# Small attention products gathered: three places per pair of heads, in the scores' PSUM buffers

## The chip, the cores and the metric

The kernel runs on one core of a Trainium2 chip. The metric is the device time of one execution in microseconds (us). TensorE multiplies matrices and writes only to PSUM; VectorE and ScalarE read PSUM and work on SBUF, the on-chip memory; GpSimd and the DMA queues do the rest. Each engine works through its own list of instructions in order, and semaphores make one wait for another. PSUM has eight banks of 2 KB per partition, and who may write into which bank when is what this change is about.

## The reference: what is computed

Attention in which a query sees only the keys that were assigned to the same of 16 cluster centroids, followed by a mixer block. Cut to what matters:

```python
# q, k, v: (4 batches, 8 heads, 768 tokens, 64); centroids: (8, 16, 64)
q_assign = np.argmax(np.einsum('bhsd,hcd->bhsc', q_n, c_n), axis=-1)   # normalized rows
k_assign = np.argmax(np.einsum('bhsd,hcd->bhsc', k_n, c_n), axis=-1)
mask = q_assign[:, :, :, None] == k_assign[:, :, None, :]
scores = scale * np.matmul(q, k.transpose(0, 1, 3, 2))
scores = np.where(mask, scores, -1000000000.0)
attn = np.exp(scores - np.max(scores, axis=-1, keepdims=True))
attn = attn / (np.sum(attn, axis=-1, keepdims=True) + 1e-09)
x = np.matmul(attn, v)                   # then heads side by side: (4, 768, 512)
# mixer: h = relu(x^T w_tok1) w_tok2; u = x + h^T; out = u + relu(u w_ch1) w_ch2
```

All inputs are 32-bit floats. The mixer is not touched by the change.

## The kernel before

Two heads are worked on together; there are 16 such pairs (4 batches x 4). A pair is done in 4 steps (`GROUPS`): two halves of the queries, and in each half two groups of three blocks of 128 keys. Step `m` makes the scores of its group, and the weighted values of the group of step `m - 1`. ScalarE takes the exponential of the scores in between, and VectorE adds the exponentials up (`add_up`).

Three pools lie in PSUM: `ps_sc` with three buffers of two banks for the scores, `ps_av` with one bank for the values, `ps_w` with one bank for everything small.

```python
def wtile(g, shape, dt, name):
    if g == 0:
        return ps_sc.tile(shape, dt, tag="sc", name=name)
    return ps_w.tile(shape, dt, tag="w", name=name)

def route_products(g, a0=0, a1=2):           # similarity to the centroids
    st, f = state[g], g % NF
    pr = wtile(g, [P, a1 - a0, NJ, QP], F32, "pr")
    for i in range(NQ):
        rows = slice(i * QP, (i + 1) * QP)
        nc.tensor.matmul(pr[rows], lhsT=cnd..., rhs=st["T"][:, a0:a1, :, rows]..., start=True, stop=True)

def route(g, a0=0, a1=2):                    # VectorE: the best centroid, as one-hot
    sc = rsmall.tile([P, NR, C], F32, name="sim")
    nc.vector.transpose(out=sc..., in_=st.pop("pr")...)
    nc.vector.reduce_max(out=mx, in_=sc, axis=AX.X)
    nc.vector.tensor_tensor(out=oh, in0=sc..., in1=mx..., op=ALU.is_ge)

def route_turn(g, a):                        # a = 1: keys, a = 0: queries
    po = wtile(g, [P, NJ, P], BF16, "po")
    for j in range(NJ):
        nc.tensor.transpose(out=po[:, j], in_=oh[:, a, j], identity=identb)
    # ... ScalarE copies po into st["ohT"][:, a]

def scores(m):
    scs = [ps_sc.tile([P, 2, 512], F32, tag="sc", name="sc") for _ in range(NG)]   # NG = 3
    for src, start in ((st["ohT"], True), (st["T"], False)):
        for i in range(NG):
            for h in range(2):
                nc.tensor.matmul(scs[i][:, h, 0:HS], lhsT=src[rows, 1, j0 + i], rhs=src[rows, 0, js],
                                 start=start, stop=not start)
    for i in range(NG):
        nc.scalar.activation(out=ex, in_=scs[i][:, :, 0:HS], func=ACT.Exp, scale=SM_SCALE)

def half_sums(hi):                           # den: sums of the exponentials over the keys
    den = st["den"] = ps_w.tile([P, 2 * HJ, QP], F32, tag="w", name="den")
    for i in range(NQ):
        nc.tensor.matmul(den[rows], lhsT=ones, rhs=acc[:, :, rows], start=True, stop=True)

def half_reciprocals(hi):                    # VectorE: transpose dent, then the reciprocal

def half_turn(hi):                           # px: the values of a half turned back
    px = st["px"] = ps_w.tile([P, HJ, P], F32, tag="w", name="px")
    for i in range(HJ):
        nc.tensor.transpose(out=px[:, i], in_=avT[:, i], identity=ident)

def half_out(hi):                            # VectorE: x = px * reciprocal
```

The scores are one sum in PSUM: the one-hot products come first (`ohT`, bf16; the same cluster or not), and the products of queries and keys (`T`, 32-bit) are added to them. The order of the steps:

```python
for m in range(last + 3):
    g, s = divmod(m, GROUPS)
    if half_at(m - 3) is not None: half_out(half_at(m - 3))
    if more and s == 0: turn(g + 1)
    if more and s == 1: route(g + 1)
    if 1 <= m <= last: add_up(m - 1)
    if m < last: scores(m)
    # ...
    if half_at(m - 2) is not None:
        half_sums(half_at(m - 2)); half_reciprocals(half_at(m - 2))
    if more and s == 2: route_turn(g + 1, 1)
    if 1 <= m <= last: values(m - 1)
    if half_at(m - 2) is not None: half_turn(half_at(m - 2))
    if more and s == 0: route_products(g + 1)
    if more and s == 2: route_turn(g + 1, 0)
    # ... loads of pair g + 2 at s == 1; every third m one step of preparing the weights
```

`half_at(m)` gives the number of the half that ends with step m (at s = 1 and s = 3). So a pair has seven places in TensorE's stream at which something small stands between the scores and the values: pr, den twice, px twice, po twice.

Of the kernel before, what the change touches and what calls it, by code (L numbers as in the profile page):

```python
# [8 lines left out]
F32 = mybir.dt.float32  # L9
# [3 lines left out]
ALU = mybir.AluOpType  # L13
# [3 lines left out]
B, H, S, D = 4, 8, 768, 64  # L17
C = 16
P = 128
NJ = S // P  # L20
# [6 lines left out]
HJ = NJ // 2  # L27
HS = HJ * P
WMAX = 512
# [18 lines left out]
def kernel(  # L48
# [52 lines left out]
    loads = pool("loads", 3, attention)  # L101
    small = pool("small", 2, attention)
    qktp = pool("qktp", 2, attention)
    work = pool("work", 7, attention)
    sums = pool("sums", 2, attention)

    routing = fast.enter_context(ExitStack())
    qkpool = pool("qkpool", 2, routing, side="right")
    rsmall = pool("rsmall", 2, routing, side="right")
    pools = {}  # L110


# [3 lines left out]
    cnT = const.tile([P, H * C], F32, name="cnT")  # L116
    cnd = const.tile([P, NF, 2, C], F32, name="cnd")
    ohs = [rsmall.tile([P, 2, NJ, P], BF16, name=f"oh{i}", bufs=1) for i in range(2)]
    rcps = const.tile([P, 2 * NPAIR, 2, HJ], F32, name="rcps")
    cells = const.tile([P, NPAIR], F32, name="cells")  # L120

    W = {
# [55 lines left out]
    def weight_steps(pool, W, names):  # L178

        def tmp(name, dt, n):
            return pool.tile([P, WMAX], dt, tag=name, name=name)[:, 0:n]

        def load_bits(src, p):  # L190
            n = p["n"] = src.shape[1]
            raw = pool.tile([P, WMAX, 2], U32, tag="raw", name="raw", bufs=3)[:, 0:n]
            nc.sync.dma_start(raw.rearrange("p n two -> p (n two)"), src.bitcast(U32))
            p["lo"], p["hi"] = raw[:, :, 0], raw[:, :, 1]

        def scalar_part(p):

            p["h"] = tmp("wh", U32, p["n"])
            nc.scalar.activation(out=p["h"].bitcast(F32), in_=p["hi"].bitcast(F32), func=ACT.Abs)
            p["up"] = tmp("wup", I32, p["n"])  # L200
            nc.scalar.activation(out=p["up"], in_=p["lo"], func=ACT.Copy, scale=float(2.0**-29))

        def rest(dst, p):

            h = p["h"]
            nc.vector.tensor_scalar(
                out=h.bitcast(F32), in0=h.bitcast(F32), scalar1=TINY, scalar2=HUGE,
                op0=ALU.max, op1=ALU.min,
            )

            nc.vector.tensor_scalar(
                out=h, in0=h, scalar1=0x07FFFFFF, scalar2=3,
                op0=ALU.bitwise_and, op1=ALU.logical_shift_left,
            )
            T = tmp("wT", U32, p["n"])
            nc.vector.scalar_tensor_tensor(  # L216
                out=T, in0=p["hi"], scalar=0xC0000000, in1=h,
                op0=ALU.bitwise_and, op1=ALU.bitwise_or,
            )
            T, up = T.bitcast(I32), p["up"]  # L220
            if len(dst.shape) == 3:
                T, up = (y.rearrange("t (p j) -> t p j", j=NJ) for y in (T, up))
            nc.gpsimd.tensor_tensor(out=dst.bitcast(I32), in0=T, in1=up, op=ALU.add)  # L223

        pieces = list(weight_pieces(W, names))
        parts = [{} for _ in pieces]
        for i in range(len(pieces) + 2):

            def step(i=i):
                if 2 <= i:  # L230
                    rest(pieces[i - 2][0], parts[i - 2])
                if 1 <= i <= len(pieces):
                    scalar_part(parts[i - 1])
                if i < len(pieces):
                    load_bits(pieces[i][1], parts[i])

            yield step
# [56 lines left out]
            return ps_sc.tile(shape, dt, tag="sc", name=name)  # L294
        return ps_w.tile(shape, dt, tag="w", name=name)

    def route_products(g, a0=0, a1=2):

        st, f = state[g], g % NF
        pr = wtile(g, [P, a1 - a0, NJ, QP], F32, "pr")  # L300
        for i in range(NQ):
            rows = slice(i * QP, (i + 1) * QP)
            nc.tensor.matmul(  # L303
                pr[rows], lhsT=cnd[:, f].rearrange("p i c -> p (i c)"),
                rhs=st["T"][:, a0:a1, :, rows].rearrange("p a j r -> p (a j) r"),
                start=True, stop=True,
            )
        st["pr"] = pr

    def route(g, a0=0, a1=2):  # L310

        st = state[g]
        NR = (a1 - a0) * NJ * 2
        sc = rsmall.tile([P, NR, C], F32, name="sim")
        nc.vector.transpose(
            out=sc.rearrange("p n c -> p (n c)"), in_=st.pop("pr").rearrange("p a j r -> p (a j r)")
        )
        mx = rsmall.tile([P, NR], F32, name="mx")  # L320
        nc.vector.reduce_max(out=mx, in_=sc, axis=AX.X)
        oh = ohs[g % 2][:, a0:a1].rearrange("p a j (h x) -> p (a j) h x", h=2)[:, :, :, 0:C]
        nc.vector.tensor_tensor(
            out=oh, in0=sc.rearrange("p (n h) c -> p n h c", h=2),
            in1=mx.rearrange("p (n h) -> p n h", h=2).unsqueeze(3).to_broadcast([P, NR // 2, 2, C]),
            op=ALU.is_ge,
        )
# [49 lines left out]
    def add_up(m):  # L377
# [1 line left out]
        st = state[g]  # L379
        e = [st["ex", qh, j0 + i] for i in range(NG)]  # L380
        if j0 == 0:
            acc = st["sum", qh] = sums.tile([P, 2, HS], F32, name="sum")
            nc.vector.tensor_tensor(out=acc, in0=e[0], in1=e[1], op=ALU.add)
            e = e[2:]
        acc = st["sum", qh]
        for ex in e:
            nc.vector.tensor_tensor(out=acc, in0=acc, in1=ex, op=ALU.add)  # L387

    def values(m):
# [9 lines left out]
                    start=(j == 0), stop=(j == NJ - 1),  # L399
                )  # L400
        if j0 == NJ - NG:
            st["avT", qh] = sums.tile([P, HJ, P], F32, name="avT")
            nc.scalar.copy(out=st["avT", qh].rearrange("p j t -> p (j t)"), in_=st.pop("av"))

    def half_sums(hi):

        g, qh = divmod(hi, 2)
        st = state[g]
        acc = st.pop(("sum", qh)).rearrange("p h (j t) -> p (h j) t", j=HJ)
        den = st["den"] = ps_w.tile([P, 2 * HJ, QP], F32, tag="w", name="den")  # L410
        for i in range(NQ):
            rows = slice(i * QP, (i + 1) * QP)
            nc.tensor.matmul(den[rows], lhsT=ones, rhs=acc[:, :, rows], start=True, stop=True)  # L413

    def half_reciprocals(hi):
        g, qh = divmod(hi, 2)
        dt = small.tile([P, 2 * HJ, QP], F32, name="dent")
        nc.vector.transpose(
            out=dt.rearrange("p n r -> p (n r)"),
            in_=state[g].pop("den").rearrange("p n r -> p (n r)"),  # L420
        )
        nc.vector.reciprocal(
            out=rcps[:, hi].rearrange("p h j -> p (h j)"), in_=dt[:, :, 0]
        )

    def half_turn(hi):
        g, qh = divmod(hi, 2)
        st = state[g]
        avT = st.pop(("avT", qh))
        px = st["px"] = ps_w.tile([P, HJ, P], F32, tag="w", name="px")  # L430
        for i in range(HJ):
            nc.tensor.transpose(out=px[:, i], in_=avT[:, i], identity=ident)  # L432

    def half_out(hi):

        g, qh = divmod(hi, 2)
        b, f = divmod(g, NF)
        nc.vector.tensor_tensor(  # L438
            out=xs[b][:, HJ * qh : HJ * qh + HJ, f * P : (f + 1) * P].rearrange(
                "p j (h d) -> p j h d", h=2  # L440
            ),
            in0=state[g].pop("px").rearrange("p j (h d) -> p j h d", h=2),
            in1=rcps[:, hi].rearrange("p h j -> p j h").unsqueeze(3).to_broadcast([P, HJ, 2, D]),
            op=ALU.mult,
        )
        if qh == 1:
            state.pop(g)


    turns = [0, 0]  # L450
# [220 lines left out]
    def fits():  # L671

        inside = const.tile([P, 3, 2 * NPAIR * 2 * HJ], F32, name="inside")
        good = const.tile([P, 3], F32, name="good")
        flat = rcps.rearrange("p n h j -> p (n h j)")
        for i, (limit, op) in enumerate(((LIMIT, ALU.is_le), (1.0 / LIMIT, ALU.is_ge))):
            nc.vector.tensor_scalar(
                out=inside[:, i], in0=flat, scalar1=limit, scalar2=None, op0=op
# [57 lines left out]
    begin()  # L736
    weights = list(weight_steps(stage, W, ("tok1", "tok2", "ch1")))
    last = NPAIR * GROUPS
    HALF = GROUPS // 2
    ends = [lambda t=t: tok1(0, t) for t in range(NT)]  # L740
    for b in range(B):
        if b + 1 < B:
            ends += [lambda b=b, t=t: tok1(b + 1, t) for t in range(NT)]
        ends += [lambda b=b, j=j: tok2(b, j) for j in range(NJ)]

    def half_at(m):

        return m // HALF if 0 <= m < last and m % HALF == HALF - 1 else None

    for m in range(last + 3):  # L750
        g, s = divmod(m, GROUPS)
        more = g < NPAIR - 1
        if half_at(m - 3) is not None:
            half_out(half_at(m - 3))
        if more and s == 0:
            turn(g + 1)
        if more and s == 1:
            route(g + 1)
        if 1 <= m <= last:
            add_up(m - 1)  # L760
        if m < last:
            scores(m)
        if m == last:
            ps_sc_stack.close()
            pools["ps_m"] = pool("ps_m", 2, space=PSUM)
        if half_at(m - 2) is not None:
            half_sums(half_at(m - 2))
            half_reciprocals(half_at(m - 2))
        if more and s == 2:
            route_turn(g + 1, 1)  # L770
        if 1 <= m <= last:
            values(m - 1)
        if half_at(m - 2) is not None:
            half_turn(half_at(m - 2))
        if more and s == 0:
            route_products(g + 1)
        if more and s == 2:
            route_turn(g + 1, 0)
        if s == 1 and g + 2 < NPAIR:
            load(g + 2)  # L780
        if m == last - GROUPS:
# [254 lines left out]
```

## Time and profile before

| | |
|---|---|
| time, median of 3 runs | 913.79 us (911.97 to 915.61) |
| span of the profiled execution | 914.3 us |
| granted TensorE clock, mean | 0.994 |
| VectorE busy | 507.3 us, 55% of the span |
| exponentials, 192 of 128 x 768 | 141.8 us busy, 812 ns each |
| sums of the exponentials, 128 + 32 of 128 x 768 | 130.1 + 30.4 us busy |
| den, 256 records of 192 columns | 17.0 us busy |
| px, 96 transposes | 17.5 us busy |
| po, 192 transposes | 17.0 us busy |
| pr, 120 records of 384 columns | 12.8 us busy |

How to read it. The page gives for each engine the time in which it was busy. Matmuls are pipelined, so the duration of one record overlaps the next; the length of a stretch of TensorE work is best read as the distance from its start to the start of what follows. A 32-bit product appears as two records. In the timeline the last bracket of a line tells how long the engine had been idle before it and what ended the wait. Shapes such as 64\*128 are the rows and columns of the array that a product uses.

### The profile page before, as it was taken

To read this page: it belongs to the slowest core of one execution; us is meant where nothing else is said; L and a number is where in the kernel's file an instruction comes from. 1 tells how busy PE (TensorE), PEld (TensorE's weight loads), DVE (VectorE), ACT (ScalarE), POOL (GpSimd) and SP (SyncE) were. 2 spreads that over 40 slices of the span, in tenths; PEclk is the share of its full clock that TensorE was granted. 3 is DMA by queue.
4 is the path that set the end of the run, shared out by engine and by line. 5 is a ranking of instruction groups with operands and counts; after the bars stand their busy time and mean duration, and the time that the engine had idled before them with its cause. 6 is when DMAs were issued, how large, how long until landed. Compare 5 with 4: busy or idle time off the path is not lost.

```text
span 914.3 us, 11630 instructions
## 1 busy us (share of the span) xinstructions
PE 895.6 (98%) x4594; PEld 533.6 (58%) x4594; DVE 507.3 (55%) x851; ACT 303.5 (33%) x515; POOL 45.0 (5%) x40
## 2 busy tenths in 40 slices
PE   7999999999999999999999899999999999999997
PEld 3444444444444444444458568677686876858676
DVE  5787787787787875577463244333443334433342
ACT  2655565565565654231130121211212012130210
POOL 1000010010010100131000000000000000000000
PEclk9999999999999999999999899999999999999999
DMA  9725426325334100240000001000010000100001
GB/s 154 157 54 107 82 70 109 80 75 99 76 85 89 62 27 1 65 143 1 0 1 1 0 1 47 23 1 1 0 47 24 0 1 12 47 12 1 1 12 61
DMA packets 112830, 41.76 MB, mean 46 GB/s; under 512 B 101632, under 2 KB 105728, under 8 KB 112768
## 3 DMA queue, kind: packets, MB, share of 16 engines
q1 hardware_dynamic: 109632, 40.55, 19.4%
q10 hardware_dynamic: 3136, 0.39, 0.4%
q8 instruction: 38, 0.62, 0.3%
q14 instruction: 24, 0.20, 0.1%
HBM read 34.64 MB, written 6.29 MB: 45 GB/s over the span
## 4 chain that ended last, share of the span: by engine, by line
PE 92%; DVE 5%; DMA 1%; issue 1%; ACT 0%; DVEq 0%
PE sc L368 16%; PE pX L652 14%; PE pX L601 14%; PE av L397 13%; PE pZ L652 7%; PE pZ L601 7%; PE ph L470 5%; PE pu L479 5%; PE pY L652 3%; PE pY L601 3%; PE px L432 2%; DVE sum L387 2%; PE po L341 2%; PE den L413 1%; PE pr L303 1%; PE pt L542 1%
## 5 line engine op out<-in xcount | busy, mean ns | idle before, releaser
L374 ACT ACTIVATE ex<-sc 128x768 f32<-128x768 f32 x192 | 141.8, 812 | 117.5 <-PE sc L368 117.5
L397 PE MATMUL av<-ex,va 128*64 128x384 f32 x768 | 138.0, 494 | 0.0
L387 DVE TENSOR_TENSOR sum<-sum,ex 128x768 f32<-128x768 f32 x128 | 130.1, 1016 | 10.1
L368 PE MATMUL sc<-qkT 64*128 64x384 f32 x768 | 134.3, 482 | 0.0
L368 PEld LDWEIGHTS sc<-qkT 64*128 64x128 f32 x768 | 71.4, 187 | 38.0
L397 PEld LDWEIGHTS av<-ex,va 128*64 128x64 f32 x768 | 49.4, 136 | 66.2 <-issue 59.8
L601 PE MATMUL pX<-uT,wc 128*128 128x384 f32 x192 | 68.8, 495 | 1.6 <-issue 1.6
L609 ACT COPY p<-pX 128x384 f32<-128x384 f32 x24 | 11.4, 475 | 153.1 <-PE pX L601 153.1
L601 PEld LDWEIGHTS pX<-uT,wc 128*128 128x128 f32 x192 | 36.7, 193 | 26.7 <-issue 3.3
L223 POOL TENSOR_TENSOR wc<-wT,wup 128x512 int32<-128x512 int32 x24 | 32.4, 1349 | 251.2 <-DVE wT L216 251.2
L368 PE MATMUL sc<-ohT 64*128 64x384 bf16 x384 | 42.6, 327 | 0.6 <-DVE ohT L344 0.6
L479 PE MATMUL pu<-h,wt 128*128 128x512 f32 x96 | 42.0, 592 | 0.0
L470 PE MATMUL ph<-x,wt 128*128 128x512 f32 x96 | 42.0, 593 | 0.0
L496 DVE TENSOR_TENSOR x<-pX,x 128x256 f32<-128x256 f32 x24 | 10.2, 424 | 55.1 <-PE pX L652 55.1
L496 DVE TENSOR_TENSOR c<-pZ,u 128x384 f32<-128x384 f32 x24 | 13.4, 557 | 46.8 <-PE pZ L601 46.8
L652 PE MATMUL pX<-w2s,hA 128*128 128x256 f32 x144 | 36.4, 390 | 0.5 <-DVE x L496 0.5
L438 DVE TENSOR_TENSOR x<-px,rcps 128x384 f32<-128x384 f32 x32 | 17.8, 556 | 33.5 <-PE px L432 33.5
L496 DVE TENSOR_TENSOR hA<-pY,p 128x384 f32<-128x384 f32 x24 | 13.4, 557 | 40.4 <-PE pY L601 40.4
L652 PE MATMUL pX<-wc,hA 128*128 128x256 f32 x144 | 35.0, 379 | 0.0
L601 PE MATMUL pZ<-uTs,w1s 128*128 128x384 f32 x96 | 35.0, 487 | 0.0
L652 PE MATMUL pX<-w2s,hS 128*128 128x256 f32 x144 | 35.0, 379 | 0.0
L652 PE MATMUL pZ<-wc,hS 128*128 128x256 f32 x144 | 35.0, 379 | 0.0
(115 smaller groups left out, 1227.0 us busy)
## 6 DMA issues: line engine op xcount, KB each, us to landing
raw<-in_moe_w_ch_dram SPq DMA_DIRECT2D x24, 512.0 KB, 3.9
qk<-in_k_dram SPq DMA_DIRECT2D x64, 96.0 KB, 4.4
va<-in_v_dram SPq DMA_DIRECT2D x16, 384.0 KB, 3.3
out_dram<-x SPq DMA_DIRECT2D x24, 256.0 KB, 2.0
qk<-in_q_dram SPq DMA_DIRECT2D x60, 96.0 KB, 3.6
raw<-in_moe_w_tok_dram SPq DMA_DIRECT2D x3, 512.0 KB, 5.8
raw<-in_moe_w_tok_dram SPq DMA_DIRECT2D x4, 384.0 KB, 4.2
qk<-in_q_dram ACTq DMA_DIRECT2D x4, 96.0 KB, 4.8
```

What stands on the lines that cost most here:

```text
L223: nc.gpsimd.tensor_tensor(out=dst.bitcast(I32), in0=T, in1=up, op=ALU.add)
L341: nc.tensor.transpose(out=po[:, j], in_=oh[:, a, j], identity=identb)
L368: nc.tensor.matmul(scs[i][:, h, 0:HS], lhsT=src[rows, 1, j0 + i], rhs=src[rows, 0, js], start=start, stop=not start,)
L374: nc.scalar.activation(out=ex, in_=scs[i][:, :, 0:HS], func=ACT.Exp, scale=SM_SCALE)
L387: nc.vector.tensor_tensor(out=acc, in0=acc, in1=ex, op=ALU.add)
L397: nc.tensor.matmul(st["av"][h * D : (h + 1) * D], lhsT=st["va"][:, h, j], rhs=ex[:, h], start=(j == 0), stop=(j == NJ - 1),)
L432: nc.tensor.transpose(out=px[:, i], in_=avT[:, i], identity=ident)
L470: nc.tensor.matmul(pf, lhsT=W["tok1"][:, j, t * P : (t + 1) * P], rhs=xs[b][:, j], start=(j == 0), stop=(j == NJ - 1),)
L479: nc.tensor.matmul(pu, lhsT=W["tok2"][:, t, j], rhs=h1s[b][:, t], start=(t == 0), stop=(t == NT - 1))
L496: nc.vector.tensor_tensor(out=dst, in0=a, in1=b, op=ALU.add)
L601: nc.tensor.matmul(psum, lhsT=A[a][:, k, c * P : (c + 1) * P], rhs=R[r][:, k], start=start and k == 0, stop=k == 1, skip_group_check=not s ...
L652: nc.tensor.matmul(psum, lhsT=h2[a][:, k, i * P : (i + 1) * P], rhs=Bw[w][:, 3 * part + k], start=start and k == 0, stop=k == 2, skip_grou ...
```

## The change

The small products of a pair are put together, each for the whole pair, and in three places: den and pr side by side after the values of step 1, px (six transposes) and the keys' po after the values of step 2, the queries' po after the values of step 3. The den and pr pair takes one of the three score buffers (two banks: one each), and px takes one too. It is meant to spare TensorE the changes between small and large products, VectorE and ScalarE some instructions, and to free the small products from the single bank of `ps_w`. The room for whole pairs in SBUF comes from fewer work buffers (6 for 7), single buffers in the routing scratch and a single `wT`.

```diff
-    work = pool("work", 7, attention)
+    work = pool("work", 6, attention)
-    rsmall = pool("rsmall", 2, routing, side="right")
+    rsmall = pool("rsmall", 1, routing, side="right")
 ...
+            bufs = 1 if name == "wT" else 2
 ...
-    def route_products(g, a0=0, a1=2):
+    def route_products(g, a0=0, a1=2, pr=None):
-        pr = wtile(g, [P, a1 - a0, NJ, QP], F32, "pr")
+        if pr is None:
+            pr = ps_sc.tile([P, (a1 - a0) * NJ * QP], F32, tag="sc", name="pr")
 ...
+    def pair_sums(g, den):
+        acc = st.pop("sum").rearrange("p i h (j t) -> p (i h j) t", j=HJ)
         for i in range(NQ):
             nc.tensor.matmul(den[rows], lhsT=ones, rhs=acc[:, :, rows], start=True, stop=True)
+    def pair_reciprocals(g):      # one transpose of 384 columns, one reciprocal of 12
+    def pair_turn(g, px):         # six transposes, three into each bank
+    def pair_out(g):              # two products, one per bank
 ...
     for m in range(last + 3):
         g, s = divmod(m, GROUPS)
+        old = g - 1 if m < last else -1
+        if s == 3 and old >= 0:
+            pair_out(old)
         if more and s == 0:
             turn(g + 1)
-        if more and s == 1:
-            route(g + 1)
+        if s == 2:
+            if old >= 0:
+                pair_reciprocals(old)
+            if more:
+                route(g + 1)
         if 1 <= m <= last:
             add_up(m - 1)
         if m < last:
             scores(m)
+        if 1 <= m <= last:
+            values(m - 1)
+        if m < last and s == 1:
+            both_w = ps_sc.tile([P, 2, 512], F32, tag="sc", name="small")
+            if old >= 0:
+                pair_sums(old, both_w[:, 0, 0:HS])
+            if more:
+                route_products(g + 1, pr=both_w[:, 1, 0:HS])
+        if m < last and s == 2:
+            if old >= 0:
+                px = ps_sc.tile([P, 2, 512], F32, tag="sc", name="px")
+                pair_turn(old, [px[:, i, 0:HS] for i in range(2)])
+            if more:
+                route_turn(g + 1, 1)
+        if more and s == 3:
+            route_turn(g + 1, 0)
 ...
+        if m == last + 1:         # the last pair: sums, reciprocals and turn, in ps_w and ps_av
```

The half-wise calls of before are taken out.

More of the change, by code (lines that the diff above doesn't have):

```diff
@@ L118 @@
     ohs = [rsmall.tile([P, 2, NJ, P], BF16, name=f"oh{i}", bufs=1) for i in range(2)]
-    rcps = const.tile([P, 2 * NPAIR, 2, HJ], F32, name="rcps")
+    rcps = const.tile([P, NPAIR, 2, 2, HJ], F32, name="rcps")
     cells = const.tile([P, NPAIR], F32, name="cells")
@@ L187, in tmp @@
         def tmp(name, dt, n):
-            return pool.tile([P, WMAX], dt, tag=name, name=name)[:, 0:n]
+            bufs = 1 if name == "wT" else 2
+            return pool.tile([P, WMAX], dt, tag=name, name=name, bufs=bufs)[:, 0:n]
         def load_bits(src, p):
@@ L317, in route @@
         nc.vector.transpose(
-            out=sc.rearrange("p n c -> p (n c)"), in_=st.pop("pr").rearrange("p a j r -> p (a j r)")
+            out=sc.rearrange("p n c -> p (n c)"), in_=st.pop("pr")
         )
@@ L381, in add_up @@
         if j0 == 0:
-            acc = st["sum", qh] = sums.tile([P, 2, HS], F32, name="sum")
+            if qh == 0:
+                st["sum"] = sums.tile([P, 2, 2, HS], F32, name="sum")
+            acc = st["sum"][:, qh]
             nc.vector.tensor_tensor(out=acc, in0=e[0], in1=e[1], op=ALU.add)
             e = e[2:]
-        acc = st["sum", qh]
+        acc = st["sum"][:, qh]
         for ex in e:
@@ L401, in values @@
         if j0 == NJ - NG:
[L402 to L407, printed above, removed]
+            if qh == 0:
+                st["avT"] = sums.tile([P, NJ, P], F32, name="avT")
+            js = slice(HJ * qh, HJ * qh + HJ)
+            nc.scalar.copy(out=st["avT"][:, js].rearrange("p j t -> p (j t)"), in_=st.pop("av"))
+    def pair_sums(g, den):
         st = state[g]
-        acc = st.pop(("sum", qh)).rearrange("p h (j t) -> p (h j) t", j=HJ)
-        den = st["den"] = ps_w.tile([P, 2 * HJ, QP], F32, tag="w", name="den")
+        acc = st.pop("sum").rearrange("p i h (j t) -> p (i h j) t", j=HJ)
+        st["den"] = den
         for i in range(NQ):
@@ L413, in half_sums @@
             nc.tensor.matmul(den[rows], lhsT=ones, rhs=acc[:, :, rows], start=True, stop=True)
[L415 to L420, printed above, removed]
-        )
[L422 to L432, printed above, removed]
@@ L434, in half_out @@
-    def half_out(hi):
-        g, qh = divmod(hi, 2)
-        b, f = divmod(g, NF)
[L438 to L447, printed above, removed]
+    def pair_reciprocals(g):
+        dt = small.tile([P, 4 * HJ, QP], F32, name="dent", bufs=1)
+        nc.vector.transpose(out=dt.rearrange("p n r -> p (n r)"), in_=state[g].pop("den"))
+        nc.vector.reciprocal(
+            out=rcps[:, g].rearrange("p i h j -> p (i h j)"), in_=dt[:, :, 0]
+        )
@@ new lines, in pair_turn @@
+    def pair_turn(g, px):
+        avT = state[g].pop("avT")
+        for i in range(NJ):
+            nc.tensor.transpose(
+                out=px[i // HJ][:, (i % HJ) * P : (i % HJ) * P + P], in_=avT[:, i], identity=ident
+            )
+        state[g]["px"] = px
+    def pair_out(g):
+        b, f = divmod(g, NF)
+        px = state[g].pop("px")
+        for qh in range(2):
+            nc.vector.tensor_tensor(
+                out=xs[b][:, HJ * qh : HJ * qh + HJ, f * P : (f + 1) * P].rearrange(
+                    "p j (h d) -> p j h d", h=2
+                ),
+                in0=px[qh].rearrange("p (j h d) -> p j h d", h=2, j=HJ),
+                in1=rcps[:, g, qh].rearrange("p h j -> p j h").unsqueeze(3)
+                .to_broadcast([P, HJ, 2, D]),
+                op=ALU.mult,
+            )
+        state.pop(g)
@@ L674, in fits @@
         good = const.tile([P, 3], F32, name="good")
-        flat = rcps.rearrange("p n h j -> p (n h j)")
+        flat = rcps.rearrange("p n i h j -> p (n i h j)")
         for i, (limit, op) in enumerate(((LIMIT, ALU.is_le), (1.0 / LIMIT, ALU.is_ge))):
@@ L738 @@
     last = NPAIR * GROUPS
-    HALF = GROUPS // 2
     ends = [lambda t=t: tok1(0, t) for t in range(NT)]
@@ L744 @@
         ends += [lambda b=b, j=j: tok2(b, j) for j in range(NJ)]
-    def half_at(m):
-        return m // HALF if 0 <= m < last and m % HALF == HALF - 1 else None
     for m in range(last + 3):
@@ L752 @@
         more = g < NPAIR - 1
-        if half_at(m - 3) is not None:
-            half_out(half_at(m - 3))
+        old = g - 1 if m < last else -1
+        if s == 3 and old >= 0:
+            pair_out(old)
         if more and s == 0:
             turn(g + 1)
-        if more and s == 1:
-            route(g + 1)
+        if s == 2:
[3 more added lines that the diff above has]
+                route(g + 1)
         if 1 <= m <= last:
@@ L765 @@
             pools["ps_m"] = pool("ps_m", 2, space=PSUM)
[L766 to L778, printed above, removed]
+        if m == last + 1:
+            pair_sums(NPAIR - 1, ps_w.tile([P, HS], F32, tag="w", name="den"))
+            pair_reciprocals(NPAIR - 1)
+            pair_turn(
+                NPAIR - 1,
+                [
+                    ps_w.tile([P, HS], F32, tag="w", name="px"),
+                    ps_av.tile([P, HS], F32, name="av"),
+                ],
+            )
+        if m == last + 2:
+            pair_out(NPAIR - 1)
         if s == 1 and g + 2 < NPAIR:
```

## The prediction

> **What bounds the kernel now.** I read the page's busy shares first, then its chain of waits, then the timeline of one head pair in the middle of the attention, with the engines TensorE, VectorE and ScalarE kept side by side. From the page:
>
> ```profile
> span 914.3 us, 11630 instructions
> PE 895.6 (98%) x4594; PEld 533.6 (58%) x4594; DVE 507.3 (55%) x851; ACT 303.5 (33%) x515; POOL 45.0 (5%) x40
> ...
> PE 92%; DVE 5%; DMA 1%; issue 1%; ACT 0%; DVEq 0%
> ```
>
> TensorE is busy 98% of the span and is 92% of the chain that ended last. So time is won only by giving TensorE less to do or fewer gaps, and every wait put into its stream is paid in full. The change touches only the attention, 15.8 to about 367 us. The timeline of one pair (start, duration, engine, line, output and input):
>
> ```profile
> 212.33 2.10 PE L368 MATMUL sc<-qkT 64*128 64x384 f32 x12
> ...
> 214.36 2.16 PE L397 MATMUL av<-ex,va 128*64 128x384 f32 x12
> ...
> 216.44 0.85 PE L303 MATMUL pr<-qkT,cnd 128*32 128x384 f32 x8
> ...
> 217.23 0.66 PE L368 MATMUL sc<-ohT 64*128 64x384 bf16 x6
> ...
> 218.72 0.57 DVE L317 STREAM_TRANSPOSE sim<-pr 128x384 f32<-128x384 f32 x1
> ...
> 219.75 0.53 PE L413 MATMUL den<-sum,ones 128*32 128x192 f32 x8
> ...
> 220.22 2.16 PE L397 MATMUL av<-ex,va 128*64 128x384 f32 x12
> ...
> 222.91 0.55 PE L432 MATMUL px<-ident,avT 128*128 128x128 f32 x3 [0.54 <-DVE dent L418]
> ...
> 223.39 0.66 PE L368 MATMUL sc<-ohT 64*128 64x384 bf16 x6
> ...
> 225.92 0.51 PE L341 MATMUL po<-identb,oh 128*128 128x128 bf16 x6
> ...
> 226.36 2.16 PE L397 MATMUL av<-ex,va 128*64 128x384 f32 x12
> ...
> 228.44 0.51 PE L341 MATMUL po<-identb,oh 128*128 128x128 bf16 x6
> ...
> 228.89 0.66 PE L368 MATMUL sc<-ohT 64*128 64x384 bf16 x6
> 228.99 0.80 ACT L346 COPY ohT<-po 128x768 bf16<-128x768 bf16 x1
> 229.38 2.10 PE L368 MATMUL sc<-qkT 64*128 64x384 f32 x12
> ...
> 232.01 0.38 DVE L418 STREAM_TRANSPOSE dent<-den 128x192 f32<-128x192 f32 x1 [3.04 <-PE den L413]
> ...
> 232.43 0.19 DVE L422 RECIPROCAL rcps<-dent 128x6 f32<-128x6 f32 x1
> ...
> 234.55 0.56 DVE L438 TENSOR_TENSOR x<-px,rcps 128x384 f32<-128x384 f32 x1 [0.38 <-PE px L432]
> ```
>
> The reader takes from it the start-to-start lengths on TensorE, which carry everything below: one-hot scores 0.50 (228.89 to 229.38), score products 2.03 (212.33 to 214.36), value products 2.08 (214.36 to 216.44), pr 0.79, den 0.47, px 0.48, po 0.44. TensorE goes from each to the next without a gap; the one it shows, 0.54 before px, is the VectorE's dent, and the same list for all pairs has three such gaps of 0.6 and one of 0.17, about 2 us in all. Two more things: no small product is followed at once by something that needs its result (the copy ohT at 228.99 is for scores that start a whole step later), and VectorE starts 0.04 to 0.07 after a TensorE group ends.
>
> **What the Trainium skill says.** "TensorEngine Tiling (Array Packing)", Key Properties: changing the tiling mode drains TensorE. The trace agrees: three px transposes follow each other every 0.11, yet the place costs 0.48, so about 0.15 lies in going in and out; po is 6 x 0.057 = 0.34 and costs 0.44. The third column of shapes gives four modes (64*128 scores, 128*64 values, 128*32 pr and den, 128*128 px and po). "TensorE: Matmul & The Clock Gate", Part 3, The mechanism: matmuls are strictly first in, first out; only weight loads are pulled ahead. So a matmul that waits for a buffer stops all behind it. "Perfetto Trace Analysis", Optimizing Tensor Performance, Matmuls: independent groups should rotate through PSUM banks so that emptying one lies beside the next group. Before, the three score buffers do just that (no wait in the trace); the change puts more work with slower readers into that rotation.
>
> **The change part by part.** A pair has four steps, s = 0 to 3, each scores, then values of the step before.
> Removed: the mode switches. Before, the four steps have 3+4+4+4 = 15 switches, after 2+3+3+3 = 11. The columns streamed are the same: den was twice 192 and is once 384, px twice 3 transposes and now 6. Step lengths after, without waits: s0 0.50+2.03+2.08 = 4.61; s1 adds den with 384 columns ahead of pr in the same mode (0.65, estimated from pr's 0.79 less the switch) and pr 0.79 = 6.05; s2 adds six transposes (about 0.75) and po 0.44 = 5.80; s3 adds po 0.44 = 5.05. Sum 21.5, against before 4 x 4.61 + 0.79 + 2 x 0.47 + 2 x 0.48 + 2 x 0.44 = 22.0. Saved about 0.48 a pair, 7 us over 15 pairs, and the 2 us of dent waits: 9 us.
>
> Added: three waits on TensorE in each pair.
> (A) den and pr lie in one score buffer, and the next scores use the three buffers in rotation, so their third tile takes that one and waits until VectorE has read both halves. In the order of instructions the transpose dent waits for TensorE and the transpose sim for nothing: dent's wait already covers the end of pr. From den's start: pr starts at 0.65 and ends at 1.50; dent 1.57 to 2.15 (384 columns: 0.58 by the sim row); reciprocal until 2.38, the next starts 0.1 after it began; sim 2.30 to 2.88; TensorE goes on at 2.94. Without the wait it reaches the third tile at 0.65 + 0.79 + 2/3 of 0.50 = 1.77. Wait 1.2.
> (B) px lies in a score buffer too, read by two products of 0.56; the first waits for all six transposes. From px's start: transposes end 0.82, products 0.87 to 1.92, TensorE goes on at 1.98; without it 0.75 + 0.44 + 0.33 = 1.52. Wait 0.45. VectorE comes to it just in time (after sim: maximum 0.55, one-hot 0.6, three sums 3.05, so 7.2 from den's start; px ends about 8.1), except in the five pairs whose weight step falls in s2: its three operations (0.42 + 0.43 + 0.69) push it 0.6 later, wait 1.05.
> (C) po for the queries moves from s2 to the end of s3, and the next step on TensorE is the next pair's scores, which need its copy as moving operand. po ends 0.51 after its start, ScalarE (idle then, the exponentials are done 1 us earlier) copies from 0.55 to 1.35, scores start at 1.40 in place of 0.44. Wait 0.96.
>
> Sum: A 14 full pairs x 1.2, and 0.45 each for the first (no den) and last (no pr) = 17.7; B 9 x 0.45 + 5 x 1.05 + 0.85 for the last pair, which has no po to cover it = 10.2; C 15 x 0.96 = 14.4. Together 42.3. Saved 9. The last pair's sums and turn now come whole after the loop, 0.65 more streamed and a 0.2 longer dent: 0.8. Net +34: 913.8 + 34 = 948; I take 947, as the first reader may overlap more than I let it.
>
> Not on the path: one work buffer less (ScalarE's exponentials then wait for sums two steps back, done in time by the times above), single buffers in the routing scratch (one engine's own order) and in the weight scratch (a step every 3 steps), fewer VectorE and ScalarE instructions (both have idle time in the pair: VectorE was busy 17.5 of 22.6).
>
> **Rivals.** (1) The mode switches are worth more than I think and the waits lie under slack: then 905. For it: it is what the change is meant for. Against: TensorE has no slack anywhere in the pair, and C is a plain chain of TensorE, ScalarE, TensorE that nothing can fill, 14 us alone. (2) Only C hurts, because dent starts as soon as den ends and px's first product after three transposes. Then A falls to about 0.65 and B to 0.1 to 0.6: 10 + 4 + 14 - 8 = +20, 934. Against it: the missing waits on the second reader. (3) VectorE becomes the bound: its work per pair is about 19.5 with a weight step and the pair gets 24 long, so no; it would show as waits of ScalarE for VectorE and give 960 or more. (4) The gaps of about 1 us make the clock fall. The Trainium skill, "TensorE: Matmul & The Clock Gate", Part 1, What's actually happening, puts the idle window at about 3.4 us, and the gaps are a third of that; in the trace the granted clock is 1.00 all through the attention, also with the gap of 0.54. Unlikely, and worth 50 us or more.
>
> **Range and chances.** The low end, 934, is rival 2; the high end, 960, has 0.15 more for each of some 43 resumptions after a wait (6 us), or VectorE late in more pairs. Faster by 2% (below 895.5) would need the whole account to be wrong: 0.02. Within 2% (to 932): only if two of the three waits are nearly nothing: 0.08. Slower: 0.90.
>
> **What would show it.** The timeline of a middle pair should be 24.0 to 24.8 long in place of 22.6; the one-hot scores at s0 should start 1.4 after po with an idle of about 0.9 put down to the ScalarE copy; in the one-hot group at s2 an idle of about 1.2 put down to sim, at s3 one of 0.5 to 1.1 put down to the output product. Matmul busy time should fall by some 7 us while idle grows by about 42. If TensorE shows no idle before the scores at s0, step C is wrong; if dent starts before pr has ended, step A; if po and px side by side still cost 1.3 together, the switch saving.

## The result and the profile after

The changed kernel takes 946.89 us (median of 6, 945.95 to 948.74) against 914.62 us (6 runs of the kernel before): ratio 1.0358, 95% interval 1.0339 to 1.0376. It is slower by 32.3 us, and the prediction said 947. From the page of the changed kernel, the span, the busy time of each engine, and the shares of the chain that ended last:

```profile
span 945.0 us, 11319 instructions
...
PE 891.6 (94%) x4466; PEld 533.4 (56%) x4466; DVE 498.9 (53%) x819; ACT 305.6 (32%) x515; POOL 44.7 (5%) x40
...
PE 89%; DVE 7%; ACT 2%; DMA 1%; issue 1%; DVEq 0%
```

TensorE's busy time fell by 4.0 us, and still the span grew by 30.7: TensorE's share fell from 98% to 94%, and VectorE and ScalarE rose from 5% and 0% of the chain to 7% and 2%. Nothing new is computed; TensorE waits. For whom, the list of waits of the changed kernel says (who waits, for whom: us in total, times, longest):

```profile
PE sc L370 <- DVE sim L319: 13.9, 15, 1.0
...
PE sc L370 <- ACT ohT L348: 13.3, 15, 0.9
...
PE sc L370 <- DVE x L441: 7.8, 15, 0.9
```

These are three waits, each in 15 pairs, all before one-hot products of the scores; the kernel before has none of them. The timeline of a pair in the middle shows each at its place (start, duration, engine, line, operation; in brackets the idle time before, and what ended it). `small` is the buffer that den and pr share, `sc<-ohT` are the one-hot products, `av` the values:

```profile
239.04 0.85 PE L418 MATMUL small<-sum,ones 128*32 128x384 f32 x8
...
239.71 0.83 PE L305 MATMUL small<-qkT,cnd 128*32 128x384 f32 x8
...
240.47 0.50 PE L370 MATMUL sc<-ohT 64*128 64x384 bf16 x4
240.61 0.58 DVE L422 STREAM_TRANSPOSE dent<-small 128x384 f32<-128x384 f32 x1 [4.95 <-PE small L305]
241.23 0.23 DVE L423 RECIPROCAL rcps<-dent 128x12 f32<-128x12 f32 x1
241.37 0.52 DVE L319 STREAM_TRANSPOSE sim<-small 128x384 f32<-128x384 f32 x1
...
241.95 0.34 PE L370 MATMUL sc<-ohT 64*128 64x384 bf16 x2 [0.98 <-DVE sim L319]
...
246.24 0.88 PE L431 MATMUL px<-ident,avT 128*128 128x128 f32 x6
...
246.95 0.50 PE L343 MATMUL po<-identb,oh 128*128 128x128 bf16 x6
247.15 1.02 DVE L441 TENSOR_TENSOR x<-px,rcps 128x384 f32<-128x384 f32 x2 [1.08 <-PE px L431]
...
247.38 0.50 PE L370 MATMUL sc<-ohT 64*128 64x384 bf16 x4
...
248.23 0.34 PE L370 MATMUL sc<-ohT 64*128 64x384 bf16 x2 [0.35 <-DVE x L441]
...
252.52 0.51 PE L343 MATMUL po<-identb,oh 128*128 128x128 bf16 x6
...
253.06 0.80 ACT L348 COPY ohT<-po 128x768 bf16<-128x768 bf16 x1 [1.58 <-PE po L343]
...
253.91 0.66 PE L370 MATMUL sc<-ohT 64*128 64x384 bf16 x6 [0.89 <-ACT ohT L348]
```

Wait A: den and pr follow each other; four of the six one-hot products run (240.47), then the last two stand until VectorE has read both halves of the buffer (sim ends at 241.89). They start at 241.95, 1.48 after the first four, where they are due after 0.33: 1.15 lost. Wait B: after px and po the same four run (247.38), and the last two stand for the two output products: 0.85 in place of 0.33, 0.52 lost. Wait C: po starts at 252.52, ScalarE's copy runs from 253.06 to 253.86, and the next pair's scores start at 253.91, 1.39 after po in place of 0.44: 0.95 lost.

A pair, from one den to the next, is 24.10 us long, in five of the pairs 24.5 to 24.6; the kernel before has 22.01 for most. In the five longer ones VectorE comes late to the output products, since three operations of a weight step stand ahead of them:

```profile
197.62 0.88 PE L431 MATMUL px<-ident,avT 128*128 128x128 f32 x6
...
198.35 0.69 DVE L217 SCALAR_TENSOR_TENSOR wT<-raw,wh 128x512 uint32<-128x512 uint32 x1
198.96 1.02 DVE L441 TENSOR_TENSOR x<-px,rcps 128x384 f32<-128x384 f32 x2
...
200.03 0.34 PE L370 MATMUL sc<-ohT 64*128 64x384 bf16 x2 [0.77 <-DVE x L441]
```

px is done at 198.50 there, but the output products start at 198.96, right behind the weight step, and TensorE's idle is 0.77 in place of 0.35. From the first scores to the first product of the mixer the attention takes 383.41 us against 351.71: 31.7 us more, where the profiled spans differ by 30.7.

### The profile page after: what moved, and what is told of

It reads as the page before. It is cut to its first block, busy times and chain, and to the rows that moved or that the text cites. A ratio compares the mean times of both kernels' runs of the same rounds, so it can differ in the third digit from the quotient of the medians.

```text
span 945.0 us, 11319 instructions
## 1 busy us (share of the span) xinstructions
PE 891.6 (94%) x4466; PEld 533.4 (56%) x4466; DVE 498.9 (53%) x819; ACT 305.6 (32%) x515; POOL 44.7 (5%) x40
## 4 chain that ended last, share of the span: by engine, by line
PE 89%; DVE 7%; ACT 2%; DMA 1%; issue 1%; DVEq 0%
PE sc L370 15%; PE pX L655 13%; PE pX L604 13%; PE av L401 13%; PE pZ L655 7%; PE pZ L604 7%; PE ph L473 4%; PE pu L482 4%; PE pY L655 3%; PE pY L604 3%; DVE x L441 2%; DVE sum L391 1%; ACT ohT L348 1%; PE small L418 1%; PE small L305 1%; PE pt L545 1%
## 5 line engine op out<-in xcount | busy, mean ns | idle before, releaser
L391 DVE TENSOR_TENSOR sum<-sum,ex 128x768 f32<-128x768 f32 x128 | 125.1, 978 | 10.6 <-ACT ex L376 0.5
L370 PE MATMUL sc<-ohT 64*128 64x384 bf16 x384 | 48.4, 329 | 36.4 <-DVE sim L319 13.9
L370 PEld LDWEIGHTS <-ohT 64*128 64x128 bf16 x384 | 15.6, 94 | 73.0 <-issue 34.7
L422 DVE STREAM_TRANSPOSE dent<-small 128x384 f32<-128x384 f32 x15 | 8.7, 583 | 76.4 <-PE small L305 71.2
L387 DVE TENSOR_TENSOR sum<-ex 128x768 f32<-128x768 f32 x32 | 32.4, 1012 | 15.7 <-ACT ex L376 15.6
L655 PE MATMUL pZ<-w2s,hS 128*128 128x256 f32 x144 | 35.0, 379 | 0.0
L655 PE MATMUL pY<-wc,hA 128*128 128x256 f32 x144 | 35.0, 379 | 0.0
```

Of the source, the lines that this page charges most:

```text
L655: nc.tensor.matmul(psum, lhsT=h2[a][:, k, i * P : (i + 1) * P], rhs=Bw[w][:, 3 * part + k], start=start and k == 0, stop=k == 2, skip_grou ...
```

## The experiments

A pair length below is the distance from the start of one pair's den (or pr) to that of the next in the timeline. The times of the kernel before, run beside each group of kernels, were 913.71 to 915.51 us.

**One wait taken away at a time.** Each of the next three moves one block of small products from behind the values of its step to between scores and values. Work, buffers and mode switches stay; the values (2.08 us) now lie between the product and whoever needs its buffer or copy.

```diff
         if m < last:
             scores(m)
+        if more and s == 3:            # c_early; a_early: the den/pr block; b_early: px and po
+            route_turn(g + 1, 0)
         if 1 <= m <= last:
             values(m - 1)
 ...
-        if more and s == 3:
-            route_turn(g + 1, 0)
```

The queries' po early (wait C):

> The changed kernel with one move: the queries' po of step 3 stands between the scores and the values of that step instead of after the values. Same products, same number of mode switches. Theory (wait C is a plain chain TensorE, ScalarE copy, TensorE with nothing beside it): the 2.08 us of values now cover the copy, 15 x 0.95 = 14.3 us go, so 932.5 us. Rival (the loss comes from the larger products and the switches, the idle only shows where they end): within 3 us of 947.

Measured 933.26 us (ratio to before 1.0207, 1.0183 to 1.0230); pairs of 23.14, each 0.96 shorter. Waits A and B stay as they were (13.9 and 7.8 us). C is the plain chain.

den and pr early (wait A):

> The changed kernel with one move: den and pr of step 1 stand between scores and values instead of after the values. Theory: the values cover dent, reciprocal and sim, wait A goes (14 x 1.15 and two of 0.4, about 17 us). VectorE also gets through with sim 2 us earlier, so that the five output products delayed by a weight step come in time: about 2 us of wait B more. 927 to 930 us. Rival (a buffer taken out of the rotation costs the same wherever its products stand): no gain over 3 us, the idle moves to another tile of the scores.

Measured 927.11 us (1.0144, 1.0127 to 1.0162). All pairs are 22.95: 1.15 shorter, and the five long ones are gone too, as VectorE is through with sim earlier.

px and the keys' po early (wait B):

> The changed kernel with one move: px and the keys' po of step 2 stand between scores and values. Theory: the values cover the two output products where VectorE is on time, wait B goes in ten pairs; in the five pairs with a weight step on VectorE ahead of them the products come so late (px itself is earlier now) that about 1 us of wait stays. 4 to 6 us gained: 941 to 943 us. Rival (wait B is the two products alone): all of its 10 us go, 937 us.

Measured 941.2 us (1.0296, 1.0275 to 1.0316). Nine of the fourteen distances from den to den are 23.6, 0.53 shorter; five stay at 24.5 to 24.6. The list of waits of this kernel:

```profile
PE sc L370 <- DVE sim L319: 13.9, 15, 1.0
PE sc L370 <- ACT ohT L348: 13.3, 15, 0.9
...
PE sc L370 <- DVE x L441: 3.9, 5, 0.9
```

The wait for the output product x is down from 15 times to 5. These five are the pairs in which VectorE comes late; the two products alone are not the whole of wait B, and the rival's 937 us is out.

**All three at once.**

> All three moves at once: every small product stands between the scores and the values of its step. Theory: the three waits lie in series on TensorE and all are covered, what stays is the saving of four mode switches a pair (0.5 us x 15) and of the 2 us of dent waits of the kernel before: 905 us, faster than both kernels. Rival (VectorE, with about 19.5 us of work per pair, becomes the bound once a pair takes 21.5 us): 910 to 918 us, with waits of TensorE or ScalarE for VectorE in the pairs with a weight step.

Measured 904.33 us (0.9894, 0.9876 to 0.9913): faster than both. One pair in its timeline:

```profile
212.74 0.85 PE L418 MATMUL small<-sum,ones 128*32 128x384 f32 x8
...
213.41 0.83 PE L305 MATMUL small<-qkT,cnd 128*32 128x384 f32 x8
...
214.16 2.16 PE L401 MATMUL av<-ex,va 128*64 128x384 f32 x12
214.30 0.58 DVE L422 STREAM_TRANSPOSE dent<-small 128x384 f32<-128x384 f32 x1 [1.90 <-PE small L305]
...
215.06 0.52 DVE L319 STREAM_TRANSPOSE sim<-small 128x384 f32<-128x384 f32 x1
...
216.25 0.66 PE L370 MATMUL sc<-ohT 64*128 64x384 bf16 x6
...
218.78 0.88 PE L431 MATMUL px<-ident,avT 128*128 128x128 f32 x6
...
219.49 0.50 PE L343 MATMUL po<-identb,oh 128*128 128x128 bf16 x6
219.69 1.02 DVE L441 TENSOR_TENSOR x<-px,rcps 128x384 f32<-128x384 f32 x2
...
219.92 2.16 PE L401 MATMUL av<-ex,va 128*64 128x384 f32 x12
...
222.01 0.66 PE L370 MATMUL sc<-ohT 64*128 64x384 bf16 x6
...
224.54 0.51 PE L343 MATMUL po<-identb,oh 128*128 128x128 bf16 x6
...
224.97 2.16 PE L401 MATMUL av<-ex,va 128*64 128x384 f32 x12
...
225.45 0.82 ACT L348 COPY ohT<-po 128x768 bf16<-128x768 bf16 x1
...
227.06 0.66 PE L370 MATMUL sc<-ohT 64*128 64x384 bf16 x6
```

After each small product the values (av) start at once, VectorE or ScalarE empties the buffer beside them, and the scores start 2.09 after the values, with no idle of TensorE in a bracket. Pairs are 21.47 to 21.56 long. The three moves alone gain 13.6, 19.8 and 5.7 us, 39.1 together; all at once gain 42.6. Most of the difference lies in the five pairs in which B's move alone gained nothing: with A's move as well, 0.53 is gained in each of them, 2.7 us. VectorE as a bound is out: TensorE has no wait for it left in the pairs.

**Is it the shared buffer? pr back in the small bank.** Only the place of pr changes; den stays in the score buffer, behind the values.

```diff
-            both_w = ps_sc.tile([P, 2, 512], F32, tag="sc", name="small")
-            if old >= 0: pair_sums(old, both_w[:, 0, 0:HS])
-            if more: route_products(g + 1, pr=both_w[:, 1, 0:HS])
+            if old >= 0:
+                den_w = ps_sc.tile([P, 2, 512], F32, tag="sc", name="small")
+                pair_sums(old, den_w[:, 0, 0:HS])
+            if more: route_products(g + 1, pr=ps_w.tile([P, HS], F32, tag="w", name="pr"))
```

> The changed kernel with pr of step 1 in the single small bank, as before the change, and den alone in the score buffer; nothing is moved in time. Theory (dent waited for the end of pr because both lie in one buffer, and TensorE for both readers): dent starts 0.07 us after den's end in place of pr's end and is read before the third score tile needs the buffer, so the idle put down to sim goes from 0.98 to nothing, 17 us gained; VectorE is not much earlier with its sums, TensorE comes 1.15 us earlier to px, so wait B grows by some 0.6 in the five pairs with a weight step: 930 to 934 us. Rival (the wait is the restart of TensorE after small products): the idle at the third tile stays above 0.5.

Measured 932.39 us (1.0192, 1.0177 to 1.0208). From its timeline:

```profile
208.33 0.85 PE L418 MATMUL small<-sum,ones 128*32 128x384 f32 x8
...
209.00 0.83 PE L305 MATMUL pr<-qkT,cnd 128*32 128x384 f32 x8
...
209.25 0.58 DVE L422 STREAM_TRANSPOSE dent<-small 128x384 f32<-128x384 f32 x1 [3.64 <-PE small L418]
...
209.76 0.66 PE L370 MATMUL sc<-ohT 64*128 64x384 bf16 x6
...
210.01 0.52 DVE L319 STREAM_TRANSPOSE sim<-pr 128x384 f32<-128x384 f32 x1
```

dent starts 0.92 after den and no longer 1.57, before pr has ended (209.83), and the six one-hot products are one unbroken piece of 0.66. Without the common buffer the wait is gone with den behind the values as before, so it was the two readers of one buffer and no restart cost. Pairs are 22.95, the five late ones 23.87: wait B grew there from 0.94 to about 1.44, as expected.

**Wait C by itself, in the kernel before.**

```diff
-        if more and s == 2:
+        if more and s == 3:
             route_turn(g + 1, 0)
```

> The kernel before the change with one part of the change alone: the queries' po made at the end of step 3 and not of step 2. Theory: wait C by itself, 15 x 0.95 = 14 us, less about 0.1 a pair because px and po now stand side by side in one mode: 926 to 928 us. Rival (in the kernel before there is slack that hides it): 914 to 918 us.

Measured 937.63 us (1.0254, 1.0238 to 1.0270): 10 us more than expected. The timeline shows a wait I had left out:

```profile
222.99 0.55 PE L432 MATMUL px<-ident,avT 128*128 128x128 f32 x3
...
223.58 0.56 DVE L438 TENSOR_TENSOR x<-px,rcps 128x384 f32<-128x384 f32 x1 [1.93 <-PE px L432]
...
224.19 0.49 PE L341 MATMUL po<-identb,oh 128*128 128x128 bf16 x6 [0.65 <-DVE x L438]
...
224.72 0.80 ACT L346 COPY ohT<-po 128x768 bf16<-128x768 bf16 x1 [3.23 <-PE po L341]
225.57 0.66 PE L368 MATMUL sc<-ohT 64*128 64x384 bf16 x6 [0.89 <-ACT ohT L346]
```

At 225.57 stands wait C with its 0.89, as in the changed kernel. Ahead of it, po waits 0.65 for the output product of VectorE (line 438): px and po share the one small bank there. The follow-up gives the queries' po a score buffer (`wtile` takes one for g = 0):

```diff
-        po = wtile(g, [P, NJ, P], BF16, "po")
+        po = wtile(g if a else 0, [P, NJ, P], BF16, "po")
```

> The kernel before the change with the queries' po at the end of step 3, as in the last look at it, but po in a score buffer in place of the single small bank. Theory (of the 23 us lost there, some 10 are po waiting in that bank for the output product to read px, seen as an idle of 0.65 before po; the rest is wait C): the idle before po goes, 0.95 - 0.1 a pair stays, 926 to 929 us. Rival (moving po to the end of step 3 costs 1.5 us a pair wherever it lies): 936 us or more.

Measured 924.62 us (1.0104, 1.0088 to 1.0119), pairs of 22.85: 22.01 + 0.95 for C - 0.10 for px and po in one mode give 22.86. The time is below the expected range. In part this is so because the waits for dent of the kernel before (2 us, three pairs of 22.61 and one of 22.18) are gone in this kernel, which I had not counted: the attention is 10.5 us longer than before, as 15 x 0.85 - 2.0 = 10.7 says. The rest of the shortfall lies outside the attention and was not taken apart. The single bank was indeed a bottleneck for products put close together, and the change was right to fear it.

**The smaller SBUF buffers.** In the kernel before:

```diff
-    work = pool("work", 7, attention)
+    work = pool("work", 6, attention)
-    rsmall = pool("rsmall", 2, routing, side="right")
+    rsmall = pool("rsmall", 1, routing, side="right")
+            bufs = 1 if name == "wT" else 2
```

> The kernel before the change with the change's smaller buffers alone: 6 work buffers for 7, single buffers in the routing scratch, one wT. Theory: none of them is waited for on the way to TensorE, 914 us, within 1. Rival (the exponentials wait for the sums two steps back): 916 us or more, with ScalarE waiting for VectorE.

Measured 915.37 us against 914.43 (ratio 1.0005, 0.9997 to 1.0014). No cost shows; by the interval it is 1.3 us at most.

**The five long pairs.** In the changed kernel, weight steps that fall into step 2 put off to step 3.

```diff
-            n = m % WEVERY == 0 or m == 1
+            n = (m % WEVERY == 0 and s != 2) or (m % WEVERY == 1 and s == 3) or m == 1
```

> The changed kernel with the weight steps that fall into step 2 put off to step 3 of the same pair; same work. Theory (in five of the pairs, 24.5 us long in place of 24.1, the three weight operations on VectorE stand ahead of the output products): all pairs 24.1 us long, 2.1 us less in all, 944 to 945.5 us. Rival (the weight loads or ScalarE's part of the step are in the way): the five longer pairs stay, or others become longer.

Measured 944.54 us (1.0321, 1.0305 to 1.0337), and all pairs are 24.10. It was the weight step. This run moves ScalarE's part of the step too; that VectorE's part was in the way is read from the lines above, in which the output products start right behind the last of its three operations.

**What a mode switch costs.** From all three moves, the keys' po of step 2 back behind the values, so that px and po stand apart:

```diff
         if m < last and s == 2:        # px, between scores and values
-            if more:
-                route_turn(g + 1, 1)
 ...
             values(m - 1)
+        if more and s == 2:
+            route_turn(g + 1, 1)
```

> All three moves, but the keys' po of step 2 after the values, so that px and po stand apart: one mode switch more a pair, nothing else. Theory (a switch costs 0.10 to 0.15 us, read from px 0.71 ahead of po and 0.81 ahead of scores): 1.5 to 2.2 us more than with all three moves. Rival (switches cost nothing and the saving came from waits): the same time.

Measured 906.56 us (0.9904, 0.9889 to 0.9920), beside 904.33 (0.9894, 0.9876 to 0.9913): the intervals overlap, the times alone do not tell. The pairs do: 21.57 or 21.58 in all of them, 0.10 to 0.11 more than 21.47. The cost is there, and small. Whether it belongs to the change of mode or to one more separate place as such, these runs do not tell apart; below it is called the cost of a switch.

**One place less still.** Both po after px in step 2, in a score buffer of their own, no small product in step 3:

```diff
-            if more:
-                route_turn(g + 1, 1)
-        if more and s == 3:
-            route_turn(g + 1, 0)
+        if more and s == 2:
+            pos = ps_sc.tile([P, 2, 1024], BF16, tag="sc", name="po")
+            for a in (1, 0):           # turn into pos[:, a], and ScalarE's copy
+                route_turn(g + 1, a, pos[:, a, ...])
```

> All three moves, and both po of a pair right after px in step 2, in a score buffer of their own, so that step 3 has no small product: one mode switch less a pair (10 in place of 11). Theory (a switch is 0.10 us): pairs of 21.36 in place of 21.47 us, 1.5 us less, 902 to 904 us. Rival (two of the three score buffers are now away at once, and the scores of step 3 wait for ScalarE's two copies): longer pairs, 906 to 915 us, with TensorE waiting for the copy ohT at step 3.

Measured 920.95 us (1.0062, 1.0047 to 1.0076): neither. TensorE does wait for the copy, but not at step 3:

```profile
208.03 0.50 PE L344 MATMUL po<-identb,oh 128*128 128x128 bf16 x6
...
208.56 0.81 ACT L351 ACTIVATE ohT<-po 128x768 bf16<-128x768 bf16 x1 [0.20 <-PE po L344]
...
209.51 0.49 PE L344 MATMUL po<-identb,oh 128*128 128x128 bf16 x6 [0.99 <-ACT ohT L351]
```

The second po waits until ScalarE has copied the first (208.56 to 209.37), because both lie in one buffer and I had written turn, copy, turn, copy. It is wait A again, in the writing direction: each half is 2 KB, a bank of its own, but in this program the writer of one half waits for the reader of the other. With all twelve turns ahead of the two copies:

```diff
-            for a in (1, 0):
-                route_turn(g + 1, a, pos[:, a, ...])
+            for a in (1, 0): route_turn(g + 1, a, po[a], copy=False)
+            for a in (1, 0): route_turn(g + 1, a, po[a], turn=False)
```

> As the last look at two places, but all twelve po transposes come before ScalarE's two copies. Theory (the wait of 0.99 before the second po came only from both po lying in one buffer whose first half ScalarE was reading): that wait goes, pairs of 21.36 us, 15 x 0.1 us less than with all three moves, 902 to 904 us. Rival (the copies, both now after the second po, hold the third score tile of step 3): a wait for the copy ohT at step 3, 905 us or more.

Measured 902.84 us (0.9876, 0.9855 to 0.9898), all pairs 21.36: the shortest pairs of the study, by the 0.11 of one switch. The interval overlaps that of all three moves; the pairs tell the two apart.

## Why the prediction was right

Point by point:

- *The gain from fewer places* was put at 0.48 us a pair. A pair with its three waits subtracted is 24.10 - 1.15 - 0.52 - 0.95 = 21.48, and with the waits really gone it is 21.47; before it was 22.01. The gain is 0.54. (The prediction's own step lengths give 22.01 - 21.51 = 0.50.) The parts: den to pr 0.67 (predicted 0.65), px to po 0.71 (0.75), pr to scores 0.76 (0.79).
- *Wait A*, 1.2 predicted, 1.15 measured. That dent would wait for the end of pr was read from the order of instructions, and shown by pr in its own bank.
- *Wait B*, 0.45 and 1.05 predicted, 0.52 and 0.94 measured. The five late pairs and their cause were right.
- *Wait C*, 0.96 predicted, 0.95 measured, alone in the kernel before as well.
- *The sum*, 42.3 predicted: 14 x 1.15 + 2 x 0.43 + 9 x 0.52 + 4.8 + 0.85 + 15 x 0.95 = 41.5. Here 0.43 is A in the first and the last pair, 4.8 is B in the five late ones, 0.85 B in the last.
- *Not on the path*: the smaller buffers, shown in the kernel before.
- *The clock*: the granted clock reads 1.00 over the attention of the changed kernel, as before; gaps of about 1 us three times in 24 did not lower it.

What was off: I said that busy time would fall by 7 us and idle grow by 42. The profile shows 4.0 (2.4 of it in the attention) and, by the list of waits, 35.0. A matmul's record reaches past the start of the next, so where the stream stops in the middle of the one-hot products, 0.17 of the stop still counts as busy (0.98 of idle for 1.15 lost). The working by start-to-start distances was not touched by it. And a small wait was missed: the second step of the first pair now follows the first with nothing between, and meets exponentials that are not done, two idles of 0.15 and 0.36. The 22.6 named as the pair before is the pair shown there, with its gap of 0.54; most are 22.01. Of the 0.8 for the last pair nothing can be seen: from the first product of the mixer to the end it is 546.5 us against 546.8, at a granted clock of 1.00 against 0.99.

That the total came out at the very number is luck. The working gave +34 and 948; 947 was taken because the first reader might start early, which it did not. Waits of 41.5 in place of 42.3, 0.5 for the small wait and a gain of 10 in place of 9 give 32, and 32.3 was measured; the kernel before came out at 914.6 in place of 913.8, which made up for the smaller rise. The mechanism and the size of each wait are what was right.

Of the rivals, the first (switches worth more, waits under slack, 905) is refuted by the three waits in the trace and by the 0.10 of a switch; 904 is reached only where the waits are covered. The second (first readers that start early) is refuted by dent at 240.61, after pr's end; the third (VectorE as the bound) by the run with all moves, which waits for it nowhere at 21.47 a pair.

## What to carry to other kernels

When TensorE is the bound, the order of its stream can be worth more than its length: put a small product whose result, or whose buffer, is needed next ahead of a long independent one, not behind it. Here the same three places cost 32 us behind the values and gain 10 ahead of them. Before putting two things into one buffer, ask who empties each half and who waits for the buffer: here the waits went by the buffer, so the first reader waited for the last writer, and the next writer for the last reader.

## What I had not expected of the hardware

That one change of array mode (with the separate place that goes with it) can be read so evenly: 0.10 to 0.11 us a pair, in both kernels in which one was added or removed alone, close to the 0.12 that the prediction reckoned (0.48 for four). Four of them are 0.42 us of the 0.54 that a pair gains; the last 0.1 was not taken apart. VectorE starts an instruction that waits for nothing before the record of the one ahead has ended, as the prediction had reckoned with 0.1: sim starts 0.14 after the reciprocal started, whose own record lasts 0.23 (241.23 and 241.37). And the end of a TensorE record hides part of a stop: 1.15 us lost read as 0.98 of idle.
